# The last two stores of an attention and gating kernel in unequal shares of rows, on two queues

## The chip, the cores and the metric

The kernel runs on one core of a Trainium2 chip. The metric is device time in microseconds (us) for one execution, the median of several runs. Inputs and output lie in the chip's memory (HBM). A core has TensorE (matrix products, into PSUM), VectorE, ScalarE and GpSimd, and SyncE, which issues transfers; ScalarE and GpSimd can issue transfers too. The transfers of all queues are carried out by the core's 16 DMA engines.

## What is computed

Inputs are q, k and v of shape (4, 8, 768, 64), that is batch, heads, tokens, head width; a sort network of 8x8 values for each batch and head; and the weights of a gated block. The reference, cut to what matters:

```python
for _ in range(5):                       # P starts as sort_net
    P = exp(P - max(P, -1))
    P = P / (sum(P, -1) + 1e-9)
    P = P / (sum(P, -2) + 1e-9)
k_sorted, v_sorted = P applied to the 8 blocks of 96 tokens of k and v
attn = softmax(q_block @ k_sorted_block.T / 8)
x = (attn @ v_sorted_block), heads side by side     # (4, 768, 512)
h = relu(x @ w_in); u, v = the two halves of h      # 512 columns each
v_n = (v - mean(v)) / sqrt(var(v) + 1e-6)
v_s = w_spatial @ v_n + b_spatial                   # mixes the tokens
out = (u * v_s) @ w_out                             # (4, 768, 512), float32
```

## The kernel before

The work is cut into 360 units with short names (`VP`, `SP`, `OP` and so on), each a small function `u_XX`. A string, `ORDER` (L18 to L51), lists them, and a loop at L776 calls them in that order. Each engine carries out its own instructions in the order in which they are emitted, and waits on semaphores for what it reads. The order is written out by hand; nothing is planned at run time. The batch elements are 0 to 3, and the units of neighbouring elements are interleaved.

The 768 tokens of one element are six tiles of 128 rows. The last product, `out`, goes through these units:

- For elements 0, 1 and 2 the tiles are handled in pairs. `OP` (L628) multiplies a pair into PSUM (L635), `OE` (L642) copies it to a buffer in SBUF by ScalarE (L115) or VectorE (L117), and `OS` (L648) stores the pair, 128 rows by two tiles by 512 columns of float32 (512 KB), by one transfer that SyncE issues (L650). There are nine pairs.
- For element 3, the last one, the tiles are handled singly, in parts. `SH` (L660) mixes the tokens (L665) and adds the bias (L671), `GH` (L673) multiplies by u (L678), `OH` (L680) multiplies by the output weights (L685), `OI` (L690) copies a tile, or half the columns of one, out of PSUM (L115 on ScalarE, L117 on VectorE), and `OJ` (L695) stores it (L697). A store of 512 columns is 256 KB, one of 256 columns 128 KB. Tiles 4 and 5 go in two halves of 256 columns. The last stores in the order are tile 1, the second half of tile 4, and tile 0.

The buffers for the pairs and for the single tiles come from one pool of eight (`ld`, L99), which the loads of q, k and v use before. The function `queue` (L108) chooses the issuer: `A` is ScalarE, `S` is SyncE. In the traces the transfers of SyncE are queue q1 and those of ScalarE q10; q8 and q14 fetch instructions.

On SyncE other things stand between the stores: the copies from `vm` to `vb` (L423), four transposes of `x` into `xT` (`XD`, L506), and a load of a flag from SBUF (L721). At the end of the program SyncE waits until all transfers have landed (L807).

Of the kernel before, what the change touches and what calls it, by code (L numbers as in the profile page):

```python
# [38 lines left out]
VP:3:A:2:2:3 AT:1:3:3:1 GT:P:1:0 VP:2:A:2:0:1 ST:2:3 AT:1:3:2:1 AT:3:3:1:1 UP:0:A:2:1:1 OP:1:1:0 ST:2:0 ST:2:1 ST:2:2  # L39
OE:A:1:0 AT:2:3:0:1 LN:2:0:6 LA:2:1 UP:0:D:2:0:0 SC:1:3:0:0 LA:2:3 SC:3:3:1:0 LA:2:2 LA:2:5 LA:2:0 OP:2:1:4 AT:1:3:0:0  # L40
AT:3:3:1:0 XD:3:1 OE:A:1:4 OP:0:1:2 LA:2:4 SC:1:3:3:0 OE:D:1:2 SC:3:3:2:0 SP:2:2:2 AT:1:3:2:0 UP:0:A:2:0:1 AT:3:3:3:0
CK VP:2:A:3:4:5 GT:D:2:2 OS:1:2 SP:1:2:1 ST:3:5 OS:1:4 XD:3:0 SP:3:2:3 SP:2:2:0 ST:3:4 CF:3 GT:D:2:1 GT:P:2:3
UP:0:A:3:1:0 VP:2:D:3:2:3 VP:3:A:3:0:1 ST:3:0 ST:3:1 ST:3:2 UP:2:A:3:0:1 GT:P:2:0 LF OP:1:2:2 ST:3:3 OE:A:2:2 LN:3:0:6
OP:0:2:0 LA:3:4 LA:3:5 OS:2:2 OE:A:2:0 UP:3:D:3:1:1 LA:3:2 LA:3:0 OP:2:2:4 LA:3:3 OE:A:2:4 LA:3:1 OS:2:4 UP:0:A:3:0:0
SH:1:3:3:0 GH:P:3:3:0 SH:2:3:0:0 GH:D:3:0:0 SH:0:3:1:0 SH:2:3:2:0 SH:3:3:1:1 GH:P:3:1:0 SH:1:3:0:1 GH:P:3:2:0 OS:1:0
GH:P:3:1:1 SH:2:3:3:1 SH:3:3:2:1 OH:1:3:2:0:512:0:4 OS:2:0 GH:P:3:0:1 GH:D:3:2:1 GH:D:3:3:1 OH:2:3:3:0:512:0:4 OS:0:4
OH:0:3:4:0:256:0:4 OI:A:3:2:0:512 OI:A:3:3:0:512 OH:3:3:5:0:256:0:4 OI:D:3:4:0:256 OI:D:3:5:0:256 OJ:3:2:0:512:S
OJ:3:3:0:512:S OJ:3:4:0:256:S OJ:3:5:0:256:A OH:2:3:5:256:512:0:4 OH:1:3:1:0:512:0:4 OH:3:3:4:256:512:0:4
OI:D:3:5:256:512 OI:A:3:1:0:512 OJ:3:5:256:512:S OI:A:3:4:256:512 OJ:3:4:256:512:S OJ:3:1:0:512:A OH:2:3:0:0:512:0:4
OI:A:3:0:0:512 OJ:3:0:0:512:S  # L50
"""  # L51


# [12 lines left out]
def kernel(  # L66
# [12 lines left out]
    nc = tc.nc  # L79

    B, H, S, D = q.shape
    NB = sort_net.shape[-1]
    BLK = S // NB
    G = S // 128
# [23 lines left out]
    def queue(eng):  # L108
        if "general" in st:
            return nc.gpsimd  # L110
        return nc.scalar if eng == "A" else nc.sync

    def copy(eng, out, in_):
        if eng == "A":
            nc.scalar.copy(out=out, in_=in_)  # L115
        else:
            nc.vector.tensor_copy(out=out, in_=in_)  # L117
# [37 lines left out]
    st = {}  # L155
    count = {"e": 0, "k": 0}

    def ld_tile(name):
        return ld.tile([128, H, G * D], BF16, name=name, tag="ld")
# [197 lines left out]
    def u_QP(eng, b, hp):  # L357

        b, hp = int(b), int(hp)
        if ("qp", b) not in st:  # L360
            st["qp", b] = ld_tile("qp").rearrange("p h c -> p (h c)").rearrange(
                "p (k g h d) -> p k g h d", k=HP, g=G, h=2)
        getattr(nc, {"P": "gpsimd", "D": "vector"}[eng]).tensor_copy(
            out=st["qp", b][:, hp].rearrange("p g h d -> p h g d"),
            in_=st["q", b][:, 2 * hp:2 * hp + 2].rearrange("p h (g d) -> p h g d", g=G),
        )

    def u_QX(b, lo, hi):
# [326 lines left out]
    def u_OJ(b, n, c0, c1, eng="S"):  # L695
        b, n, c0, c1 = (int(x) for x in (b, n, c0, c1))
        queue(eng).dma_start(out=out[b, n * 128:(n + 1) * 128, c0:c1], in_=st["o1", b, n, c0])  # L697

    def u_CK():
        nc.vector.memset(bad, 0.0)  # L700
        over = lambda col, rows, in_, op, bound, test: (
            nc.vector.tensor_reduce(out=ends[0:rows, col:col + 1], in_=in_, axis=AX.X, op=op),
            nc.vector.tensor_scalar(
                out=bad[0:rows, col:col + 1], in0=ends[0:rows, col:col + 1],
                scalar1=bound, scalar2=None, op0=test),
        )
        recs = rec_all.rearrange("p n h i -> p (n h i)")
        over(0, BLK, recs, ALU.max, 1.0 / SUM_LO, ALU.is_gt)
        over(1, BLK, recs, ALU.min, 1.0 / SUM_HI, ALU.is_lt)
        over(2, BH, first[:, 0:NB], ALU.max, SUM_HI, ALU.is_gt)  # L710
        over(3, BH, first[:, 0:NB], ALU.min, SUM_LO, ALU.is_lt)
        over(4, BH, first[:, NB:2 * NB], ALU.min, COL_LO, ALU.is_lt)
# [99 lines left out]
```

## Time and profile before

| what | value |
|---|---|
| median of 3 runs | 157.59 us |
| lowest, highest run | 157.57, 157.9 us |
| the profiled execution | 158.23 us |
| its span | 156.4 us |
| outside the span | 1.8 us |
| TensorE busy | 147.1 us (94%) |
| VectorE busy | 120.4 us (77%) |
| ScalarE busy | 81.5 us (52%) |
| GpSimd busy | 36.8 us (24%) |
| granted TensorE clock | 0.999 |

The span runs from the first to the last instruction of one profiled execution, and times inside it are counted from its start. A group's line gives the source line, the engine, the operation, the tiles that it writes and reads with their shapes, and the count. In a timeline the first two numbers are start and length. A transfer has an issue, the short time that the issuing engine's queue needs for it, and a landing, the time from that issue until the semaphore of the whole transfer has come. A transfer's packets are spread over the DMA engines; the row of "DMA" digits gives their mean busy share in 40 equal slices of the window, and "GB/s" what they moved. Packets carry no engine's number.

### The profile page before, as it was taken

To read this page: it belongs to the slowest core of one execution; us is meant where nothing else is said; L and a number is where in the kernel's file an instruction comes from. 1 tells how busy PE (TensorE), PEld (TensorE's weight loads), DVE (VectorE), ACT (ScalarE), POOL (GpSimd) and SP (SyncE) were. 2 spreads that over 40 slices of the span, in tenths; PEclk is the share of its full clock that TensorE was granted. 3 is DMA by queue.
4 is the path that set the end of the run, shared out by engine and by line. 5 is a ranking of instruction groups with operands and counts; after the bars stand their busy time and mean duration, and the time that the engine had idled before them with its cause. 6 is when DMAs were issued, how large, how long until landed. Compare 5 with 4: busy or idle time off the path is not lost.

```text
span 156.4 us, 3976 instructions
## 1 busy us (share of the span) xinstructions
PE 147.1 (94%) x1650; PEld 89.7 (57%) x1665; DVE 120.4 (77%) x270; ACT 81.5 (52%) x112; POOL 36.8 (24%) x43
## 2 busy tenths in 40 slices
PE   6998898989999999999999999999999999999970
PEld 2355776844686669557655465555565545555640
DVE  4778699849997798479898889899969796747530
ACT  3466898867889504876556034556443025540230
POOL 7923855624000040052000000400000340006500
PEclk9999999999999999999999999999999999999999
DMA  2999999999999999990026445600569300349082
GB/s 76 264 204 204 205 204 205 207 219 239 274 209 203 204 204 204 244 198 4 0 41 198 79 160 96 114 0 4 101 235 71 67 0 0 134 151 379 13 307 105
DMA packets 27653, 23.57 MB, mean 151 GB/s; under 512 B 7280, under 2 KB 24688, under 8 KB 27632
## 3 DMA queue, kind: packets, MB, share of 16 engines
q0 software_dynamic: 14352, 11.80, 47.6%
q1 hardware_dynamic: 12992, 11.10, 26.4%
q10 hardware_dynamic: 288, 0.39, 0.7%
q8 instruction: 14, 0.23, 0.6%
q14 instruction: 7, 0.06, 0.1%
HBM read 24.78 MB, written 6.29 MB: 199 GB/s over the span
## 4 chain that ended last, share of the span: by engine, by line
PE 91%; DVE 2%; ACT 2%; issue 1%; DVEq 0%; ACTq 0%
PE ps L609 15%; PE ps L597 14%; PE ps L554 13%; PE ps L635 10%; PE ps L226 7%; PE ps L488 5%; PE ps L665 5%; PE ps L442 4%; PE ps L383 4%; PE ps L314 4%; PE ps L685 3%; PE ps L410 2%; PE ps L518 2%; PE ps L531 1%; DVE kt L117 1%
## 5 line engine op out<-in xcount | busy, mean ns | idle before, releaser
L447 ACT ACTIVATE ex<-ps 96x768 bf16<-96x768 f32 x32 | 24.8, 805 | 8.7 <-PE ps L442 8.6
L625 POOL TENSOR_TENSOR gt<-z,u_sb 128x768 bf16<-128x768 f32 x6 | 9.8, 1641 | 79.0 <-DVE z L615 61.2
L609 PE MATMUL ps<-wspT,v_sb 128*128 128x384 bf16 x144 | 25.1, 326 | 0.0
L597 PE MATMUL ps<-xT,w_in_sb 128*128 128x384 bf16 x128 | 23.5, 326 | 0.0
L554 PE MATMUL ps<-w_in_sb,xT 128*128 128x512 bf16 x87 | 22.1, 380 | 1.2 <-issue 0.8
L496 DVE TENSOR_TENSOR x_sb<-ps,rec_all 96x512 bf16<-96x512 f32 x32 | 22.0, 687 | 1.1
L609 PEld LDWEIGHTS <-v_sb 128*128 128x128 bf16 x144 | 13.5, 98 | 8.9
L571 DVE BATCH_NORM_STATS2 stats<-v_sb 128x6 f32<-128x512 bf16 x24 | 16.3, 678 | 2.0 <-ACT v_sb L121 1.5
L115 ACT COPY o_sb<-ps 128x1024 f32<-128x1024 f32 (+2 forms) x12 | 9.7, 816 | 15.2 <-PE ps L685 10.2
L635 PE MATMUL ps<-w_out_sb,gt 128*128 128x512 bf16 x68 | 16.7, 379 | 0.2
L615 DVE TENSOR_TENSOR z<-ps,b_bc 128x768 f32<-128x768 f32 x12 | 11.4, 952 | 7.0 <-PE ps L609 6.8
L121 ACT ACTIVATE u_sb<-ps 128x768 bf16<-128x768 f32 x12 | 9.7, 810 | 13.1 <-PE ps L597 13.0
L597 PEld LDWEIGHTS <-w_in_sb 128*128 128x128 bf16 x128 | 11.6, 98 | 7.4
L554 PEld LDWEIGHTS <-xT 128*128 128x128 bf16 x96 | 8.6, 98 | 10.0 <-issue 1.0
L121 ACT ACTIVATE v_sb<-ps 128x1024 bf16<-128x1024 f32 (+1 forms) x9 | 8.8, 976 | 9.4 <-PE ps L554 9.4
L488 PEld LDWEIGHTS <-ex 96*128 96x128 bf16 x256 | 10.6, 97 | 3.5
L488 PE MATMUL ps<-vb,ex 96*128 96x65 bf16 x256 | 12.1, 193 | 0.0
L226 PE MATMUL ps<-warm 128*128 128x512 bf16 x35 | 10.6, 460 | 1.3 <-DVE warm L199 1.3
L635 PEld LDWEIGHTS <-gt 128*128 128x128 bf16 x72 | 6.7, 98 | 7.2
L115 ACT CAST kt<-ps 128x768 bf16<-128x768 f32 x9 | 6.9, 800 | 6.5 <-PE ps L383 6.5
L442 PE MATMUL ps<-qT,kt 64*128 64x96 bf16 x256 | 9.3, 204 | 0.5 <-DVE kt L117 0.4
L442 PEld LDWEIGHTS <-kt 64*128 64x128 bf16 x256 | 6.2, 94 | 5.8 <-issue 3.9
(94 smaller groups left out, 208.2 us busy)
## 6 DMA issues: line engine op xcount, KB each, us to landing
out_dram<-o_sb SPq DMA_DIRECT2D x9, 512.0 KB, 3.6
k_in<-in_k_dram POOLq DMA_DIRECT2D x4, 768.0 KB, 23.3
v_in<-in_v_dram POOLq DMA_DIRECT2D x4, 768.0 KB, 22.4
vb<-vm SPq DMA_DIRECT2D x24, 99.0 KB, 5.8
q_in<-in_q_dram POOLq DMA_DIRECT2D x3, 768.0 KB, 29.6
ws_in<-in_moe_w_spatial_dram POOLq DMA_DIRECT2D x2, 576.0 KB, 22.8
w_in_sb<-in_moe_w_in_dram POOLq DMA_DIRECT2D x2, 512.0 KB, 24.1
q<-in_q_dram SPq DMA_DIRECT2D x1, 768.0 KB, 4.6
```

Source lines behind the costliest of these rows:

```text
L115: nc.scalar.copy(out=out, in_=in_)
L121: nc.scalar.activation(out=out, in_=in_, func=AF.Relu)
L226: nc.tensor.matmul(t[:, 0, 0:int(w)], lhsT=warm[:, 0:128], rhs=warm[:, 0:int(w)], start=True, stop=True)
L442: nc.tensor.matmul(t[:, hh, 0:HW].rearrange("p (g x) -> p g x", g=G)[:, :, ii * TB:(ii + 1) * TB], lhsT=kT[rows, i * BLK:i * BLK + 128], r ...
L447: nc.scalar.activation(out=e_tile(b, hp, ih).rearrange("p h (x g) -> p h x g", g=G), in_=t[0:BLK, :, 0:HW].rearrange("p h (g x) -> p h x g ...
L488: nc.tensor.matmul(t[:, hh, ii * VW:ii * VW + D + 1], lhsT=e[:, c:c + 128], rhs=vb[b % 2][:, ih * NI + ii, 2 * hp + hh, 0:D + 1], start=Tr ...
L496: nc.vector.tensor_mul(out=x_sb[:, hp].rearrange("p i (h d) -> p h i d", h=2), in0=tv[:, :, :, 0:D], in1=_raw_ap(rec, 0, [rec.ap[0], [NI, ...
L554: nc.tensor.matmul(t[:, x, :], lhsT=st["xT", b][:, n // 3, kc, (n % 3) * 128:(n % 3 + 1) * 128], rhs=w_in_sb[:, kc, DH:DFF], start=(kc == ...
L571: nc.vector.bn_stats(out=stats, in_=st["v_sb", b, n])
L597: nc.tensor.matmul(t[:, x, 0:HW], lhsT=w_in_sb[:, kc, mc * 128:(mc + 1) * 128], rhs=st["xT", b][:, ih, kc, :], start=(kc == 0), stop=(kc = ...
L609: nc.tensor.matmul(t[:, x, 0:HW], lhsT=st["v_sb", b, n][:, mc * 128:(mc + 1) * 128], rhs=wspT[:, 3 * x:3 * x + 3, n, :], start=(n == 0), s ...
L635: nc.tensor.matmul(t[:, x, :], lhsT=st["gt", b, mc][:, (n0 + x) * 128:(n0 + x + 1) * 128], rhs=w_out_sb[:, mc, :], start=(mc == 0), stop=( ...
```

## The change

Nothing of what is computed changes. In element 3, the second half of tile 4 is stored by two transfers, rows 0 to 99 by SyncE and rows 100 to 127 by ScalarE, and tile 0 by two, rows 0 to 119 by SyncE and 120 to 127 by ScalarE (new unit `OR`). The first half of tile 5 is now stored by SyncE, not ScalarE. The store of tile 1 by ScalarE stands ahead of ScalarE's copy of the second half of tile 4, and no longer behind it. Six of the nine pairs of elements 0 to 2 are stored by two transfers of SyncE, rows 0 to 119 and 120 to 127 of both tiles (new unit `OT`). The unit `QP`, which the order doesn't name, calls the helper `copy` now. The diff, with the lines of the order wrapped anew only left out where nothing else differs:

```diff
-CK VP:2:A:3:4:5 GT:D:2:2 OS:1:2 SP:1:2:1 ST:3:5 OS:1:4 XD:3:0 SP:3:2:3 SP:2:2:0 ST:3:4 CF:3 GT:D:2:1 GT:P:2:3
...
-OP:0:2:0 LA:3:4 LA:3:5 OS:2:2 OE:A:2:0 UP:3:D:3:1:1 LA:3:2 LA:3:0 OP:2:2:4 LA:3:3 OE:A:2:4 LA:3:1 OS:2:4 UP:0:A:3:0:0
-SH:1:3:3:0 GH:P:3:3:0 SH:2:3:0:0 GH:D:3:0:0 SH:0:3:1:0 SH:2:3:2:0 SH:3:3:1:1 GH:P:3:1:0 SH:1:3:0:1 GH:P:3:2:0 OS:1:0
-GH:P:3:1:1 SH:2:3:3:1 SH:3:3:2:1 OH:1:3:2:0:512:0:4 OS:2:0 GH:P:3:0:1 GH:D:3:2:1 GH:D:3:3:1 OH:2:3:3:0:512:0:4 OS:0:4
-OH:0:3:4:0:256:0:4 OI:A:3:2:0:512 OI:A:3:3:0:512 OH:3:3:5:0:256:0:4 OI:D:3:4:0:256 OI:D:3:5:0:256 OJ:3:2:0:512:S
-OJ:3:3:0:512:S OJ:3:4:0:256:S OJ:3:5:0:256:A OH:2:3:5:256:512:0:4 OH:1:3:1:0:512:0:4 OH:3:3:4:256:512:0:4
-OI:D:3:5:256:512 OI:A:3:1:0:512 OJ:3:5:256:512:S OI:A:3:4:256:512 OJ:3:4:256:512:S OJ:3:1:0:512:A OH:2:3:0:0:512:0:4
-OI:A:3:0:0:512 OJ:3:0:0:512:S
+CK VP:2:A:3:4:5 GT:D:2:2 OT:1:2:0:120 OT:1:2:120:128 SP:1:2:1 ST:3:5 OT:1:4:0:120 OT:1:4:120:128 XD:3:0 SP:3:2:3
...
+GT:P:2:0 LF OP:1:2:2 ST:3:3 OE:A:2:2 LN:3:0:6 OP:0:2:0 LA:3:4 LA:3:5 OT:2:2:0:120 OT:2:2:120:128 OE:A:2:0 UP:3:D:3:1:1
...
+SH:0:3:1:0 SH:2:3:2:0 SH:3:3:1:1 GH:P:3:1:0 SH:1:3:0:1 GH:P:3:2:0 OT:1:0:0:120 OT:1:0:120:128 GH:P:3:1:1 SH:2:3:3:1
+SH:3:3:2:1 OH:1:3:2:0:512:0:4 OT:2:0:0:120 OT:2:0:120:128 GH:P:3:0:1 GH:D:3:2:1 GH:D:3:3:1 OH:2:3:3:0:512:0:4
+OT:0:4:0:120 OT:0:4:120:128 OH:0:3:4:0:256:0:4 OI:A:3:2:0:512 OI:A:3:3:0:512 OH:3:3:5:0:256:0:4 OI:D:3:4:0:256
+OI:D:3:5:0:256 OJ:3:2:0:512:S OJ:3:3:0:512:S OJ:3:4:0:256:S OJ:3:5:0:256:S OH:2:3:5:256:512:0:4 OH:1:3:1:0:512:0:4
+OH:3:3:4:256:512:0:4 OI:D:3:5:256:512 OI:A:3:1:0:512 OJ:3:5:256:512:S OJ:3:1:0:512:A OI:A:3:4:256:512
+OR:3:4:256:512:S:0:100 OR:3:4:256:512:A:100:128 OH:2:3:0:0:512:0:4 OI:A:3:0:0:512 OR:3:0:0:512:S:0:120
+OR:3:0:0:512:A:120:128
...
+    def u_OT(b, n0, r0, r1):
+        b, n0, r0, r1 = (int(x) for x in (b, n0, r0, r1))
+        queue("S").dma_start(
+            out=out[b].rearrange("(c p) n -> p c n", p=128)[r0:r1, n0:n0 + 2, :], in_=st["o", b, n0][r0:r1])
+
+    def u_OR(b, n, c0, c1, eng, r0, r1):
+        b, n, c0, c1, r0, r1 = (int(x) for x in (b, n, c0, c1, r0, r1))
+        queue(eng).dma_start(out=out[b, n * 128 + r0:n * 128 + r1, c0:c1], in_=st["o1", b, n, c0][r0:r1])
```

More of the change, by code (lines that the diff above doesn't have):

```diff
@@ L41 @@
 AT:3:3:1:0 XD:3:1 OE:A:1:4 OP:0:1:2 LA:2:4 SC:1:3:3:0 OE:D:1:2 SC:3:3:2:0 SP:2:2:2 AT:1:3:2:0 UP:0:A:2:0:1 AT:3:3:3:0
-CK VP:2:A:3:4:5 GT:D:2:2 OS:1:2 SP:1:2:1 ST:3:5 OS:1:4 XD:3:0 SP:3:2:3 SP:2:2:0 ST:3:4 CF:3 GT:D:2:1 GT:P:2:3
-UP:0:A:3:1:0 VP:2:D:3:2:3 VP:3:A:3:0:1 ST:3:0 ST:3:1 ST:3:2 UP:2:A:3:0:1 GT:P:2:0 LF OP:1:2:2 ST:3:3 OE:A:2:2 LN:3:0:6
-OP:0:2:0 LA:3:4 LA:3:5 OS:2:2 OE:A:2:0 UP:3:D:3:1:1 LA:3:2 LA:3:0 OP:2:2:4 LA:3:3 OE:A:2:4 LA:3:1 OS:2:4 UP:0:A:3:0:0
-SH:1:3:3:0 GH:P:3:3:0 SH:2:3:0:0 GH:D:3:0:0 SH:0:3:1:0 SH:2:3:2:0 SH:3:3:1:1 GH:P:3:1:0 SH:1:3:0:1 GH:P:3:2:0 OS:1:0
-GH:P:3:1:1 SH:2:3:3:1 SH:3:3:2:1 OH:1:3:2:0:512:0:4 OS:2:0 GH:P:3:0:1 GH:D:3:2:1 GH:D:3:3:1 OH:2:3:3:0:512:0:4 OS:0:4
-OH:0:3:4:0:256:0:4 OI:A:3:2:0:512 OI:A:3:3:0:512 OH:3:3:5:0:256:0:4 OI:D:3:4:0:256 OI:D:3:5:0:256 OJ:3:2:0:512:S
-OJ:3:3:0:512:S OJ:3:4:0:256:S OJ:3:5:0:256:A OH:2:3:5:256:512:0:4 OH:1:3:1:0:512:0:4 OH:3:3:4:256:512:0:4
-OI:D:3:5:256:512 OI:A:3:1:0:512 OJ:3:5:256:512:S OI:A:3:4:256:512 OJ:3:4:256:512:S OJ:3:1:0:512:A OH:2:3:0:0:512:0:4
-OI:A:3:0:0:512 OJ:3:0:0:512:S
+CK VP:2:A:3:4:5 GT:D:2:2 OT:1:2:0:120 OT:1:2:120:128 SP:1:2:1 ST:3:5 OT:1:4:0:120 OT:1:4:120:128 XD:3:0 SP:3:2:3
+SP:2:2:0 ST:3:4 CF:3 GT:D:2:1 GT:P:2:3 UP:0:A:3:1:0 VP:2:D:3:2:3 VP:3:A:3:0:1 ST:3:0 ST:3:1 ST:3:2 UP:2:A:3:0:1
+GT:P:2:0 LF OP:1:2:2 ST:3:3 OE:A:2:2 LN:3:0:6 OP:0:2:0 LA:3:4 LA:3:5 OT:2:2:0:120 OT:2:2:120:128 OE:A:2:0 UP:3:D:3:1:1
+LA:3:2 LA:3:0 OP:2:2:4 LA:3:3 OE:A:2:4 LA:3:1 OS:2:4 UP:0:A:3:0:0 SH:1:3:3:0 GH:P:3:3:0 SH:2:3:0:0 GH:D:3:0:0
+SH:0:3:1:0 SH:2:3:2:0 SH:3:3:1:1 GH:P:3:1:0 SH:1:3:0:1 GH:P:3:2:0 OT:1:0:0:120 OT:1:0:120:128 GH:P:3:1:1 SH:2:3:3:1
[5 more added lines that the diff above has]
+OR:3:0:0:512:A:120:128
 """
@@ L362, in u_QP @@
                 "p (k g h d) -> p k g h d", k=HP, g=G, h=2)
-        getattr(nc, {"P": "gpsimd", "D": "vector"}[eng]).tensor_copy(
-            out=st["qp", b][:, hp].rearrange("p g h d -> p h g d"),
-            in_=st["q", b][:, 2 * hp:2 * hp + 2].rearrange("p h (g d) -> p h g d", g=G),
+        copy(
+            eng, st["qp", b][:, hp].rearrange("p g h d -> p h g d"),
+            st["q", b][:, 2 * hp:2 * hp + 2].rearrange("p h (g d) -> p h g d", g=G),
         )
```

## The prediction

> **What bounds the kernel now.** I read the page's head and chain first, then the last 16 us of the chain, then what SyncE waits for at the end, then the DMA table in narrow windows.
>
> ```profile
> span 156.4 us, 3976 instructions
> PE 91%; DVE 2%; ACT 2%; issue 1%; DVEq 0%; ACTq 0%
> ```
> ```profile
> 146.62 4.95 PE ps L685 x30
> 151.56 0.02 issue
> 151.58 0.58 ACT o_sb L115
> ```
> ```profile
> SPq L807 <- DMA out_dram<-o_sb: 1.7, 3, 1.0
> ```
>
> TensorE carries the chain to 151.56; the change touches no matmul. The last copy out of PSUM runs to 151.58 + 0.58 = 152.16. From there to the span's end at 156.4 are 4.24 us in which no engine computes: the last store is issued, moves and lands, and SyncE waits for it (L807). The change works on these 4.24 us. First the last store, then an early one of the same size:
>
> ```profile
> out_dram<-o_sb SPq DMA_DIRECT2D x1, 256.0 KB, 3.3
> L697 SPq DMA_DIRECT2D out_dram<-o_sb x1: 332/332/332, 152.2 to 152.2; - x1
> ```
> ```profile
> out_dram<-o_sb SPq DMA_DIRECT2D x1, 256.0 KB, 2.0
> L697 SPq DMA_DIRECT2D out_dram<-o_sb x1: 345/345/345, 147.9 to 147.9; - x1
> ```
>
> The first lands 2.0 us after its issue, the last 3.3 us after, at 152.2 + 3.3 = 155.5; another 0.9 us pass to 156.4. So 1.3 us of the end are lag. The stretches say whose (start:end, length, the five engines, clock, DMA share, GB/s):
>
> ```profile
> 151.90:153.00 1.10, 0.00 (x0) 0.00 (x0) 0.00 (x0) 0.27 (x1) 0.00 (x0) 1.00 0.91 317
> 153.00:153.80 0.80, 0.00 (x0) 0.00 (x0) 0.00 (x0) 0.00 (x0) 0.00 (x0) 1.00 0.90 323
> 153.80:155.10 1.30, 0.00 (x0) 0.00 (x0) 0.00 (x0) 0.00 (x0) 0.00 (x0) 1.00 0.08 32
> ```
>
> Until 153.8 the 16 DMA engines are 90% busy; then 0.08, which is 1.3 of 16. Closer, from 154.38 on:
>
> ```profile
> DMA  2000200002000200020000200020000200000000
> GB/s 114 0 0 0 114 0 0 0 0 114 0 0 0 114 0 0 0 114 0 0 0 0 114 0 0 0 114 0 0 0 0 114 0 0 0 0 0 0 0 0
> DMA packets 9, 0.02 MB, mean 23 GB/s; under 512 B 1, under 2 KB 1, under 8 KB 9
> ```
>
> Eight packets of 2 KB, 0.08 us apart, and a tiny one: that is one DMA engine (X below) doing alone its eight rows of the last store, 128 rows / 16. It ends at about 155.03; the landing at 155.5 is 0.47 later. Why X is late:
>
> ```profile
> q10 hardware_dynamic: 111, 0.20, 48.7%
> q1 hardware_dynamic: 138, 0.12, 34.1%
> q8 instruction: 1, 0.02, 5.9%
> q14 instruction: 1, 0.01, 2.1%
> ```
>
> In 151.9 to 153.0 one 16 KB fetch of instructions (q8) took 5.9% of 16 engines for 1.1 us: 1.04 us of one engine, in the middle of the stores. It delays by about as much as X is late. A second lag shows where the stores of the pairs end (144.6 to 145.4):
>
> ```profile
> GB/s 205 410 205 614 410 205 103 103 103 103 102 102 0 0 0 0 0 0 0 102 0 0 0 0 0 102 0 0 0 102 0 0 0 102 0 0 0 0 819 0
> q8 instruction: 1, 0.02, 7.5%
> ```
>
> Again one engine goes on alone from about 144.9, to 145.36, and the bin in which it ends (819) holds the next 16 KB fetch. I read this as the same X: its fetch starts as its stores are through. The inference is not proven by the rows, which carry no engine numbers.
>
> **The change part by part.** *The last store, 120 and 8 rows.* One engine has eight rows of a 128-row store (above), so 120 rows are 15 engines' worth, and 8 rows are one each for eight engines. If X is the one left out, its tail from 154.38 goes; if the 100 + 28 rows of the store before it also miss X, so do that store's rows, done before 154.38. The other engines were through at 153.8 and take one row more, 0.08 us. A sentence on the rule: the Trainium skill, DMA: Bandwidth & Descriptors, section "Why a DMA increments its semaphore by 16 and not by 1", says a copy from SP or ACT uses the largest number of engines up to 16 that divides its slowest dimension, and the lowest-numbered ones: 15, 8, 10 and 14 here, so engine 15 would get nothing of the last two stores. No row of before shows it. The section "Latency and other measured facts" of that page calls engines 7 and 15 the usually late ones; if X were 7, the first rival below would hold.
>
> *The order on ScalarE.* The copies and issues now:
>
> ```profile
> 150.76 0.38 ACT L115 COPY o_sb<-ps 128x256 f32<-128x256 f32 x1
> 150.90 0.34 ACTq L697 DMA_DIRECT2D out_dram<-o_sb  x1
> 151.58 0.58 ACT L115 COPY o_sb<-ps 128x512 f32<-128x512 f32 x1 [0.44 <-PE ps L685]
> ```
>
> The store of tile 1 stands behind the 256-column copy and is issued at 150.90 while that copy runs; ScalarE then idles 0.44 us for TensorE. After the change the order is copy 1, store 1, copy 4, share of store 4, copy 0. Store 1 waits for copy 1 as now: 150.90 + 0.34 = 151.24. Copy 4 is behind it: 151.24 + 0.38 = 151.62. The 28-row share waits for copy 4: 151.66 + 0.34 = 152.00. Copy 0 then starts at 152.00, not 151.58, ends at 152.58, and both shares of the last store are issued at 152.62, 0.42 later than now. That an issue holds back the next copy isn't shown by a row (the one above is followed by an idle wait anyway): bounds 0 and 0.42; the queue works in order, so I take 0.42. An issue of fewer rows may cost other than 0.33: by the store rows 0.33 to 0.40, so 0.07 at most; I take 0.33.
>
> *Landing.* An undisturbed 256 KB store took 2.0; I add 0.08 for the extra row: 152.62 + 2.08 = 154.7, 0.8 before the 155.5 of now. A floor stands beside it: the store of tile 1 stays at 128 rows, so X keeps its rows.
>
> ```profile
> out_dram<-o_sb ACTq DMA_DIRECT2D x1, 256.0 KB, 3.7
> L697 ACTq DMA_DIRECT2D out_dram<-o_sb x1: 338/338/338, 150.9 to 150.9; - x1
> ```
>
> It lands at 150.9 + 3.7 = 154.6 now and is still issued at 150.9. So what is late next is both at once, 154.6 and 154.7. If the fetch comes at another time the floor can fall to the undisturbed 154.2 to 154.3.
>
> *Store 3:5 moved from ScalarE to SyncE.* ScalarE idled there; SyncE has its next store 0.3 us later. I take 0, at most 0.07 for the store behind it, which is not the last.
>
> *Six pairs in 120 + 8.* Six more issues on SyncE. Its stores and what follows them there:
>
> ```profile
> 113.98 0.90 SPq L650 DMA_DIRECT2D out_dram<-o_sb  x2
> ```
> ```profile
> SPq L506 <- DVE ends L702: 4.3, 1, 4.3
> ```
> ```profile
> xT<-x_sb SPq DMA_TRANSPOSE x1, 5.3
> ```
> ```profile
> 124.54 1.47 PE L597 MATMUL ps<-xT,w_in_sb 128*128 128x384 bf16 x8
> ```
> ```profile
> 133.57 0.38 SPq L650 DMA_DIRECT2D out_dram<-o_sb  x1
> ```
> ```profile
> 138.32 3.11 SPq L650 DMA_DIRECT2D out_dram<-o_sb  x4
> 147.86 4.67 SPq L697 DMA_DIRECT2D out_dram<-o_sb  x6
> ```
>
> Two pairs at 113.98 become four issues, 0.9 longer. The transpose queued behind them (L506) waited 4.3 us for VectorE anyway; 3.4 are left. If it were late it would matter: it lands at 117.92 + 5.3 = 123.2 and TensorE reads xT at 124.54, so 1.3 us more are covered. The pair at 133.57 has 4 us to the next store. At 138.32 four issues become seven in a gap of 6.4 us before 147.86; at the longest of these issues (1.25, where the queue is backed up) three more are 3.7. Their bytes are the same; an engine with a double share takes 18 rows in place of 16 of each pair, an eighth more of 5 us, 0.6, landing near 146.5 where the buffer is next written at 148.1. So I cost the pairs at 0; each issue that lost its cover would cost 0.4. Their second store per buffer adds a wait to the copies that reuse it, with a satisfied count: below 0.05 each.
>
> *Sum.* Landing 155.5 to 154.7, -0.8 (last copy +0.42, lag -1.3, row +0.08); the 0.9 behind it stays. Span 155.6; the profiled execution would go from 158.23 (1.8 outside the span) to 157.4. The median of the runs is 0.64 below that execution; taking the same -0.8 from 157.59 gives **156.8**.
>
> **The rivals.** *The late engine is in the shares.* If X is one of the first eight, it gets 9 rows of the last store and 12 of the 1 KB rows before, in place of 8 and 8: one at 0.08 and four at about 0.04, +0.24. If its queue has also run dry by 153.4 (as when the fetch slips behind store 1), the 0.42 of the later copy is paid too with the old lag of 3.3. It decides from the moment that X's queue is empty when the last store arrives: 152.62 + 3.3 = 155.9, 157.59 + 0.42 = 158.0, with the rows 158.25; slower. For it: no row says which engine X is. Against: both tails are of one engine among sixteen with equal shares, first by 0.46 us and then by 1.2, and where all have eight rows I expect the one that is dealt the last rows, 120 to 127, to be the one that ends last; this is a guess from two tails, and my 0.73 below rests on it.
>
> *The shares change nothing.* The rows are still dealt to X. X would come to the last store at 154.38 as now, behind which the 0.42 hides, and end at 155.03: 157.6. The Trainium skill, same page, section "Rules for kernel authors", advises against this sort of split: two transfers on disjoint partitions use the same 16 engines, and several issuers save only issue time. The 16 engines 90% busy until 153.8 agree with it; the single engine after 153.8 speaks against its weight here, since no bandwidth is short there.
>
> *A neighbour takes over.* The stretch after 153.8 held 1.3 engines, so a second one was late too, by about 0.4. With nine rows of the last store it would land at 155.1: 157.2. That lies in my forecast's range.
>
> **How the numbers follow.** Forecast (with the neighbour) 0.73, its own range 156.3 (landing 1.3 earlier, no delay) to 157.2. No change 0.13, at 157.6. Slower 0.14, at 158.0. A measurement here tells 0.2%, 0.3 us, from no change. Range 156.3 to 157.8: it takes in the forecast and no change and leaves the slower rival out.
>
> **What would show it.** Right: after the last copy the DMA share falls to zero with no stretch of one engine alone; the last stores land about 2.1 after issue; ScalarE's last copy starts near 152.0. Wrong: a lone engine with 2 KB packets past 154.4, or a landing still 3 us after the issue. The pairs' tail at 145 should lose its lone engine; if a gap of TensorE appears near 124.5 or 148, the pairs were not free. If the last copy still starts at 151.58, the issue on ScalarE held nothing back.

## The result and the profile after

The changed kernel takes longer: the ratio of its time to that of the kernel before is 1.0061, with a 95% interval of 1.0046 to 1.0076 (medians 158.83 and 157.64 us). One of the 13 executions of the changed kernel ran at a granted clock of 0.564 and took 251.38 us; it counts in the median and not in the ratio. A second measurement of the same kernel, among the experiments below, gave 1.0025 (1.0007 to 1.0043). So it loses 0.4 to 1.0 us; the forecast was a gain of 0.8.

The head of its page, then ScalarE's timeline at the end (start, length, engine, line, what; in brackets the idle time before):

```profile
span 156.7 us, 4003 instructions
```
```profile
150.27 0.58 ACT L117 COPY o_sb<-ps 128x512 f32<-128x512 f32 x1 [1.59 <-PE ps L687]
150.89 0.39 ACTq L699 DMA_DIRECT2D out_dram<-o_sb  x1
151.38 0.37 ACT L117 COPY o_sb<-ps 128x256 f32<-128x256 f32 x1 [0.52 <-ACT o_sb L117]
151.78 0.65 ACTq L708 DMA_DIRECT2D out_dram<-o_sb  x1
152.53 0.58 ACT L117 COPY o_sb<-ps 128x512 f32<-128x512 f32 x1 [0.78 <-DMA out_dram<-o_sb]
153.14 0.31 ACTq L708 DMA_DIRECT2D out_dram<-o_sb  x1
```

TensorE ends where it did, at 151.5. The copy of tile 0 starts at 152.53, not at 151.58. It stands behind the 28-row share's issue, 151.78 + 0.65 = 152.43; the release that the row names is a transfer whose semaphore ScalarE checks in between, for 0.02 us. That semaphore's earlier transfers had landed by 146.8, so the issue is what the copy waited out. The last chain of the same profile shows the steps that have entered it:

```profile
150.89 0.39 ACTq L699
151.28 0.05 issue
151.32 0.02 ACTq L117
151.34 0.04 issue
151.38 0.38 ACT o_sb L117
151.76 0.02 issue
151.78 0.65 ACTq L708
152.43 0.04 issue
152.47 0.02 ACTq L117
152.49 0.04 issue
152.53 0.58 ACT o_sb L117
```

ScalarE's issues (ACTq) are on the path that sets the end; before, TensorE was on it to 151.56. Then the last store, and the DMA stretches after it (the columns before the clock are the idle engines; the last two are DMA share and GB/s):

```profile
out_dram<-o_sb SPq DMA_DIRECT2D x1, 240.0 KB, 2.6
L708 SPq DMA_DIRECT2D out_dram<-o_sb x1: 338/338/338, 153.1 to 153.1; - x1
```
```profile
153.90:154.40 0.50, 0.00 (x0) 0.00 (x0) 0.00 (x0) 0.00 (x0) 0.00 (x0) 0.66 0.80 164
154.40:154.90 0.50, 0.00 (x0) 0.00 (x0) 0.00 (x0) 0.00 (x0) 0.00 (x0) 0.50 0.82 229
154.90:155.30 0.40, 0.00 (x0) 0.00 (x0) 0.00 (x0) 0.00 (x0) 0.00 (x0) 0.50 0.49 184
155.30:156.70 1.40, 0.00 (x0) 0.00 (x0) 0.00 (x0) 0.00 (x0) 0.00 (x0) 0.50 0.00 0
```

The long tail of one engine is gone: the share falls from 0.82 over 0.49 to nothing, and the landing takes 2.6, not 3.3. One reason is in the instruction fetch, in the stretch from 151.2 to 152.5:

```profile
q8 instruction: 1, 0.02, 5.7%
```

This is the same 16 KB packet as before, but it ran from 151.29 to 152.47 and was through 0.66 us ahead of the last store's issue. Before, it ran from 151.94 to 152.98 and ended 0.79 behind that issue.

But look at the speed. Before, a share of 0.90 moved 323 GB/s, 359 for a full share; here 0.80 moves 164 and 0.82 moves 229, 205 and 279 for a full share. The DMA engines are nearly as busy and move 0.57 to 0.78 as much for it.

So in these two profiles the last issue is 0.95 later and the landing 0.65 shorter: +0.3 net, 156.4 to 156.7. The medians differ by more. The profiled execution of before, 158.23, lies 0.6 above its median, that of the changed kernel 0.3 below its own. What makes the loss 0.4 us in one measurement and 1.0 in the other isn't settled.

### The profile page after: what moved, and what is told of

Same layout as the page of the kernel before. It is cut to its first block, busy times and chain, and to the rows that moved or that the text cites. A ratio compares the mean times of both kernels' runs of the same rounds, so it can differ in the third digit from the quotient of the medians.

```text
span 156.7 us, 4003 instructions
## 1 busy us (share of the span) xinstructions
PE 148.8 (95%) x1665; PEld 89.8 (57%) x1665; DVE 120.4 (77%) x270; ACT 81.7 (52%) x112; POOL 36.8 (23%) x43
## 4 chain that ended last, share of the span: by engine, by line
PE 90%; ACT 3%; DVE 3%; issue 1%; ACTq 1%; DVEq 0%
PE ps L611 15%; PE ps L599 14%; PE ps L556 14%; PE ps L637 10%; PE ps L228 7%; PE ps L667 5%; PE ps L490 5%; PE ps L444 4%; PE ps L385 4%; PE ps L316 4%; PE ps L687 2%; PE ps L412 2%; PE ps L520 2%; DVE x_sb L498 1%; PE ps L533 1%; ACT o_sb L117 1%
## 5 line engine op out<-in xcount | busy, mean ns | idle before, releaser
L556 PE MATMUL ps<-w_in_sb,xT 128*128 128x512 bf16 x96 | 22.8, 380 | 0.0
L228 PE MATMUL ps<-warm 128*128 128x512 bf16 x36 | 11.2, 479 | 1.3 <-DVE warm L201 1.3
L497 DVE RECIPROCAL rec_all<-ps 96x8 f32<-96x8 f32 x32 | 6.3, 196 | 4.3 <-PE ps L490 4.0
```

Of the source, the lines that this page charges most:

```text
L228: nc.tensor.matmul(t[:, 0, 0:int(w)], lhsT=warm[:, 0:128], rhs=warm[:, 0:int(w)], start=True, stop=True)
L556: nc.tensor.matmul(t[:, x, :], lhsT=st["xT", b][:, n // 3, kc, (n % 3) * 128:(n % 3 + 1) * 128], rhs=w_in_sb[:, kc, DH:DFF], start=(kc == ...
```

## Experiments

Three theories. A: the loss is the last copy behind ScalarE's issues. B: transfers on fewer than 16 engines move slowly. C: the six pairs cost it. Three more, X, D and S, came out of the traces; the expectations below say what they mean. A quoted text is what was expected before the run. The table counts from the end of TensorE's last matmul in each kernel's own profile, in us: the start of the last copy, the issue of the last store (its larger share), SyncE's last check of a transfer, the end of the span. "112+16" and the like are rows.

| kernel | last copy | last issue | last check | end | ratio, 95% interval |
|---|---|---|---|---|---|
| before | 0.04 | 0.65 | 3.92 | 4.88 | 1 |
| changed | 0.99 | 1.60 | 4.22 | 5.18 | 1.0061 (1.0046 to 1.0076) |
| g1_again | 0.99 | 1.60 | 4.22 | 5.17 | 1.0025 (1.0007 to 1.0043) |
| e1_last | 0.04 | 0.65 | 4.37 | 5.33 | 1.0020 (1.0011 to 1.0029) |
| e2_pairs | 0.04 | 0.65 | 3.98 | 4.93 | 1.0004 (0.9995 to 1.0012) |
| e3_whole4 | 0.12 | 0.73 | 3.61 | 4.56 | 1.0003 (0.9993 to 1.0012) |
| e4_order | 0.10 | 0.72 | 4.16 | 5.12 | 1.0013 (1.0002 to 1.0025) |
| f1_behind | 0.12 | 0.74 | 3.75 | 4.70 | 1.0009 (0.9997 to 1.0021) |
| f2_thirteen | 0.12 | 0.74 | 3.82 | 4.77 | 1.0002 (0.9992 to 1.0012) |
| f3_seven | 0.04 | 0.65 | 3.81 | 4.76 | 0.9992 (0.9981 to 1.0003) |
| f4_sixteen | 1.46 | 2.07 | 4.55 | 5.51 | 1.0042 (1.0027 to 1.0057) |
| g2_store1 | 0.05 | 0.86 | 3.57 | 4.52 | 0.9995 (0.9983 to 1.0006) |
| g3_112 | 0.04 | 0.65 | 3.81 | 4.77 | 0.9999 (0.9988 to 1.0009) |
| h1_relief | 0.05 | 0.84 | 3.86 | 4.81 | 0.9996 (0.9987 to 1.0006) |

**e1_last**: before, with the last store alone in shares.

```diff
-OJ:3:0:0:512:S
+OR:3:0:0:512:S:0:120 OR:3:0:0:512:A:120:128
```

> The kernel before with one part of the change: the last store (tile 0) in shares of 120 rows by SyncE and 8 rows by ScalarE. Theory A (the change loses because ScalarE's last copy waits behind two issues on its own queue; the shares themselves gain): the last copy stays at 151.6, no DMA engine is left alone with the last store's rows, the last store lands 2.1 to 2.6 us after its issue at 152.2, total 156.9 to 157.2. Theory B (transfers on fewer than 16 engines move slowly): the last copy at 151.6 too, but the landing takes 3.3 us or more, total 157.6 to 158.0. Theory C (the six pairs cost the time): the shares do nothing, 157.6.

Measured 1.0020, slower, though the copy is not late. The DMA table from 153.86 to 154.60 of its profile, and SyncE's wait at the end:

```profile
DMA  3000020002000200002000200020002000000000
DMA packets 10, 0.02 MB, mean 22 GB/s; under 512 B 2, under 2 KB 2, under 8 KB 10
```
```profile
SPq L816 <- DMA out_dram<-o_sb: 2.1, 1, 2.1
```

Eight packets of 2 KB from one engine alone, as before: the late engine has eight rows of the 120. It is not the one that is left out. (That it is the same engine as before can't be read, since packets carry no engine's number.) The landing is 3.3 again. And there is a new loss: SyncE waits 2.1 us in one piece, and the last check comes 0.42 after the landing (4.37 against 0.65 + 3.3 = 3.95). That made theory D, for f3_seven. The total, 158.0, is at the upper end of what theory B expected.

**e2_pairs**: before, with the six pairs in shares (`OS:1:2` to `OT:1:2:0:120 OT:1:2:120:128`, and so on).

> The kernel before with the six pairs stored as 120 and 8 rows and nothing else. Theories A and B: the issues are covered, 157.6. Theory C (the pairs cost it): 158.2 to 158.6, with a gap of TensorE or a late transpose before 146. If the pairs' lone engine at 145 goes, the engine that fetches instructions is the one left out by 120 rows.

Measured 1.0004: theory C falls. But one pair moves alone, with nothing beside it, in 133.5 to 136.5, and so gives the price of a share. First the kernel before, then e2_pairs, the same 256 rows of 2 KB:

```profile
DMA packets 272, 0.52 MB, mean 175 GB/s; under 512 B 16, under 2 KB 16, under 8 KB 272
q1 hardware_dynamic: 272, 0.52, 46.2%
```
```profile
DMA packets 279, 0.52 MB, mean 175 GB/s; under 512 B 23, under 2 KB 23, under 8 KB 279
q1 hardware_dynamic: 279, 0.52, 64.3%
```

The packets took 46.2% of 16 engines for 3 us whole, 64.3% as 120 and 8 rows: 64.3 / 46.2 = 1.39 times the DMA time for the same bytes; f3_seven has the same 64.3% there. Theory B has a size now. The tiny packets, one for each engine that takes part, are 16 before and 23 = 15 + 8 after. That is what the rule of the Trainium skill says that the prediction named (DMA: Bandwidth & Descriptors, "Why a DMA increments its semaphore by 16 and not by 1"); the trace agrees.

The expectation named a sign: the lone engine at the end of the pairs should go if 120 rows leave out the engine that fetches. It stayed. At a share of 0.07 and 0.06, one engine of sixteen still moves pairs after 146.4:

```profile
146.40:146.70 0.30, 0.30 (x3) 0.18 (x2) 0.27 (x2) 0.00 (x0) 0.19 (x1) 1.00 0.07 27
146.70:147.30 0.60, 0.60 (x5) 0.25 (x4) 0.54 (x2) 0.49 (x1) 0.00 (x0) 1.00 0.06 24
```

**e3_whole4**: the changed kernel with tile 4's second half stored whole.

```diff
-OR:3:4:256:512:S:0:100 OR:3:4:256:512:A:100:128
+OJ:3:4:256:512:S
```

> The changed kernel, but the second half of tile 4 is stored whole by SyncE, not as 100 and 28 rows; everything else stays. Theory A: only store 1 is left ahead on ScalarE, the last copy starts at about 151.75 instead of 152.53, total 0.7 to 0.8 under the changed kernel, 157.2 to 157.9. Theory B (few engines are slow): the last store still has 120 and 8 rows, so most of the loss stays, 158.2 or more. Theory C: 158.6.

Measured 1.0003. ScalarE's timeline:

```profile
150.21 0.39 ACTq L698 DMA_DIRECT2D out_dram<-o_sb  x1
150.70 0.86 ACT L116 COPY o_sb<-ps 128x256 f32<-128x256 f32 x2 [0.52 <-ACT o_sb L116]
151.59 0.55 ACTq L707 DMA_DIRECT2D out_dram<-o_sb  x1
```

The copies of tiles 4 and 0 run back to back again (x2, no gap). The one issue that is left ahead of the last copy costs 0.1. The second issue is gone, and with it the loss of the changed kernel, while the pairs and the 120 + 8 rows are kept. That fits theory A; but the shares of tile 4 are gone too, and f1_behind tells the two apart.

**e4_order**: before, with the new order and every store whole (`OJ:3:1:0:512:A OI:A:3:4:256:512 OJ:3:4:256:512:S`, and `OJ:3:5:0:256:S`).

> The kernel before with only the change of order: store 1 ahead of the copy of tile 4's second half on ScalarE, and the first half of tile 5 stored by SyncE; all stores whole. Theory A: the last copy starts at 151.75, 0.2 later, but the lone engine sets the end as before: 157.6 (157.5 to 157.8). Theories B and C: 157.6.

Measured 1.0013. The copy is 0.1 late, not 0.2, but the total, 157.9, is above the 157.5 to 157.8 expected. Its last store had an unusual issue:

```profile
L696 SPq DMA_DIRECT2D out_dram<-o_sb x1: 994/994/994, 152.1 to 152.1; - x1
```

0.99 against 0.33 for the same store before. I come back to this under f4_sixteen.

**f1_behind**: the changed kernel with the 28-row share issued behind the last copy.

```diff
-OR:3:4:256:512:A:100:128 OH:2:3:0:0:512:0:4 OI:A:3:0:0:512
+OH:2:3:0:0:512:0:4 OI:A:3:0:0:512 OR:3:4:256:512:A:100:128
```

> The changed kernel with one thing moved: ScalarE issues the 28-row share of tile 4 behind the copy of tile 0, not ahead of it. Every store has the same shares. Theory A (the issue holds back the copy): the last copy starts within 0.1 us of TensorE's last matmul as before, not 1.0 us after it, and the total falls by 0.8 to 1.0 from the changed kernel, to 157.5 to 157.8. Theory B (few engines are slow): the shares still cost it, 158.3 or more.

Measured 1.0009. Its timeline:

```profile
151.14 0.86 ACT L116 COPY o_sb<-ps 128x256 f32<-128x256 f32 x2 [0.53 <-ACT o_sb L116]
151.54 1.03 ACTq L707 DMA_DIRECT2D out_dram<-o_sb  x2
```

Same transfers, same shares, one instruction moved: the copies close up, and the two issues run beside the copy. This shows theory A without a change in what moves. The copy comes 0.87 earlier than in the changed kernel and the last check only 0.47, because the landing is 3.0 again and not 2.6. In time the run is 0.8 us under the changed kernel's first measurement and 0.25 under g1_again, where the two intervals overlap. The shares bring no gain either way.

**f2_thirteen**: f1_behind with the last store cut at row 104.

```diff
-OR:3:0:0:512:S:0:120 OR:3:0:0:512:A:120:128
+OR:3:0:0:512:S:0:104 OR:3:0:0:512:A:104:128
```

> As the kernel f1_behind, but the last store is cut at row 104, not 120: 104 rows by SyncE and 24 by ScalarE. Theory X (the DMA engine that fetches instructions is not reached by shares of 100, 28 or 104 rows but is reached by 120, as the packets of the first runs count): nothing of the last two stores is left to the late engine; the lone tail goes, 156.8 to 157.2. If the late engine is among the first thirteen, or if there is no such engine, 157.5 to 157.9.

Measured 1.0002: no gain. In the stretches of its profile no engine stays alone:

```profile
153.20:153.80 0.60, 0.00 (x0) 0.00 (x0) 0.00 (x0) 0.00 (x0) 0.00 (x0) 1.00 0.76 232
153.80:154.40 0.60, 0.00 (x0) 0.00 (x0) 0.00 (x0) 0.00 (x0) 0.00 (x0) 1.00 0.35 126
154.40:155.00 0.60, 0.00 (x0) 0.00 (x0) 0.00 (x0) 0.00 (x0) 0.00 (x0) 1.00 0.00 0
```

The end is a slope, not one engine's tail. That fits an X that 104 rows miss, but it doesn't show it: the 16 KB fetch also came 0.6 us earlier than in f1_behind, counted from TensorE's end. And 13 engines have ten rows each or eight, in slow packets, and end hardly sooner than X did (last check 3.82 against 3.92).

**f3_seven**: e1_last with seven pairs in shares, so that eight transfers are added, not one.

> The kernel before with the last store as 120 and 8 rows (as e1_last) and seven pairs as 120 and 8 rows, so that eight transfers are added and not one. Theory D (at the end SyncE waits for its transfers' semaphores in a fixed order, each check 0.06 us; with one added transfer the last store's semaphore stands eight checks ahead of the end, with eight added it stands last): 0.4 less than e1_last, 157.5 to 157.7. If the 0.3 of e1_last are due to the shares themselves, 158.0.

Measured 0.9992 against 1.0020 for e1_last, with the same last store: 0.44 us (0.2 to 0.7 by the two intervals), the size that theory D gave. SyncE's wait at the end is in three pieces again:

```profile
SPq L817 <- DMA out_dram<-o_sb: 1.9, 3, 1.1
```

In the traces SyncE makes twelve checks at the end, 0.06 us apart where nothing is waited for, in a fixed order, and the transfers take eight semaphores in turn, which the last eight checks read. One transfer more shifts the last store to a place with seven checks behind it, 7 x 0.06 = 0.42; eight more shift it back. The six pairs of the change, with its two more shares, make eight. These runs show no other use of them.

**f4_sixteen**: the changed kernel with tile 4 cut at row 112 (`OR:3:4:256:512:S:0:112 OR:3:4:256:512:A:112:128`).

> The changed kernel with the store of tile 4's second half cut at row 112, not 100: 112 and 16 rows, whose counts divide by sixteen. The order on ScalarE stays. If an issue by ScalarE takes longer for a share that doesn't fill sixteen engines, ScalarE's issue takes 0.34 instead of 0.65 us and the last copy comes 0.3 earlier, total 158.2 to 158.4 (less what the late engine's seven or eight rows add). If it takes longer because SyncE issues at the same moment, 0.65 stays, and the total is 158.5 to 158.9.

Measured 1.0042. ScalarE's timeline:

```profile
151.23 1.12 ACTq L707 DMA_DIRECT2D out_dram<-o_sb  x1
152.45 0.58 ACT L116 COPY o_sb<-ps 128x512 f32<-128x512 f32 x1 [1.25 <-issue]
```

Both expectations were missed: the issue took 1.12 and the copy came 1.46 after TensorE, not 0.7 or 1.0. The longer issue again moves the copy by as much, which is theory A once more. What sets an issue's length is left open: 0.28 to 1.12 for the shares at the end. The long ones, 1.12 here (16 rows on sixteen engines) and 0.99 in e4_order (128 rows), may wait for room on the late engine; that is argued and no run tests it. Nor is the other rival settled, that an issue is longer when the other queue issues at the same moment. In the changed kernel both pairs of shares were issued together:

```profile
L708 SPq DMA_DIRECT2D out_dram<-o_sb x2: 319/328/338, 151.8 to 153.1; - x2
L708 ACTq DMA_DIRECT2D out_dram<-o_sb x2: 308/478/648, 151.8 to 153.1; - x2
```

ScalarE's issue took 0.65 beside SyncE's first one, and 0.31 beside its second.

**g1_again**: the changed kernel once more.

> The changed kernel once more, unchanged, for a second trace of its end. Theory A: the last copy starts 0.9 to 1.5 us after TensorE's last matmul because ScalarE's issue of the 28-row share is ahead of it, whatever the rest does; total 158.4 to 158.8. If the first trace was an outlier, the copy starts within 0.3.

```profile
151.21 0.65 ACTq L707 DMA_DIRECT2D out_dram<-o_sb  x1
151.95 0.59 ACT L116 COPY o_sb<-ps 128x512 f32<-128x512 f32 x1 [0.78 <-DMA out_dram<-o_sb]
```

The same 0.65 and the same 0.99 after TensorE. The copy is late in the same way again; the total, 158.2, came out lower than expected.

**g2_store1**: before, with store 1 in 104 and 24 rows (`OR:3:1:0:512:A:0:104 OR:3:1:0:512:S:104:128`) and seven pairs in shares.

> The kernel before with store 1 (tile 1, not one of the last two) in shares of 104 rows by ScalarE and 24 by SyncE, and seven pairs as 120 and 8 so that the last store's semaphore stays last at the end. Theory X (the late engine is one that 104 rows don't reach): it has 8 rows of 2 KB less behind its fetch, its tail ends 0.4 to 0.6 earlier, 157.0 to 157.3. If relieving one engine is worth nothing because the split rows move slowly themselves: 157.5 to 157.8.

Measured 0.9995, no difference that can be told. Its stretches:

```profile
153.20:153.60 0.40, 0.00 (x0) 0.00 (x0) 0.00 (x0) 0.00 (x0) 0.00 (x0) 1.00 0.62 236
153.60:154.10 0.50, 0.00 (x0) 0.00 (x0) 0.00 (x0) 0.00 (x0) 0.00 (x0) 1.00 0.10 37
```

The end comes a third of a microsecond sooner in this profile (last check 3.57 against 3.92), though SyncE's issue of the 24 rows took 0.74 and put the last one off by 0.2. A gain of 0.3 in one trace and none in twelve runs: inconclusive.

**g3_112**: f3_seven with the last store cut at row 112 (`OR:3:0:0:512:S:0:112 OR:3:0:0:512:A:112:128`).

> The kernel f3_seven (last store in two shares, seven pairs in two) with the last store cut at row 112, not 120: both shares fill sixteen engines. Theory S (rows that are dealt in another way than 128 over sixteen move slowly): the 2 KB packets of the last store take well over the 84 ns of the whole store in both, mean 110 to 150, and the total is that of f3_seven, 157.4 to 157.8. If only a count under sixteen is slow: 84 to 90 ns here and 0.3 less, 157.1 to 157.4.

```profile
152.40:152.90 0.50, 0.00 (x0) 0.00 (x0) 0.00 (x0) 0.00 (x0) 0.00 (x0) 1.00 0.88 260
152.90:153.40 0.50, 0.00 (x0) 0.00 (x0) 0.00 (x0) 0.00 (x0) 0.00 (x0) 1.00 0.85 279
```

Between the two expectations: 260 / 0.88 = 295 and 279 / 0.85 = 328 GB/s for a full share, where the whole store has 323 / 0.90 = 359 and the changed kernel 205 and 279. A 2 KB packet of the last stores took 102 ns in the mean here, 114 in f3_seven and 91 in the kernel before. Filling sixteen engines helps, but a split store stays slower than a whole one, so theory B's few engines are not all of it. Why the rows move slowly is open. The total is that of before.

**h1_relief**: the last store whole, the two ahead of it in shares that miss X, six pairs in shares.

> The last store whole again (128 rows by SyncE); the two stores ahead of it in shares that miss the late engine: tile 1 as 104 rows by ScalarE and 24 by SyncE, the second half of tile 4 as 100 rows by SyncE and 28 by ScalarE, the last issued behind the copy of tile 0; six pairs in two, so that the last store's semaphore stays last. Theory X with theory S (the gain is in relieving the late engine while the last rows themselves move at 84 to 91 ns): 0.2 to 0.4 less than g2_store1, 157.1 to 157.3. If issues of shares eat it again (SyncE's of 24 rows took 0.74), 157.5 to 157.8.

Measured 0.9996. SyncE's issue of the 24 rows again took 0.73, and the end is that of before. The gain expected from relieving X didn't come. So no version here beats the kernel before by more than its interval.

## Why the prediction was wrong

**The sum.** Two terms of the forecast were mis-sized. The later copy cost 0.95 us where it took 0.42, and landing got shorter by 0.65 where it took 1.3, less 0.08 for a row. In the two profiles that turns -0.8 into +0.3. With only one of the two put right, a gain of 0.2 to 0.3 would have been left.

**What bounds the kernel, right.** The end is issue, movement and landing of the last stores, and one engine's tail of 1.2 us is in it. That this engine is the one that fetched stays an inference. The packets of the trace fit it: each begins 4 ns before the end of the one ahead of it on its engine, and followed back so, the last engine's row begins at 153.03, 0.05 after the fetch ended.

**The order on ScalarE: the term that was mis-sized.** The prediction took "0.42" for the later copy, from whole stores' issues of 0.34. The mechanism was right, an issue holds back the next copy (f1_behind, f4_sixteen), but it cost 0.95. The 28-row issue took 0.65, not 0.34, so the bound that the prediction gave for a smaller share, 0.07 more at most, failed by itself. Store 1's issue took 0.39, and copy 4 started at 151.38, not 151.24; and 0.10 lies between the issue and the copy. 0.42 + 0.31 + 0.14 + 0.10 = 0.97, and two steps between were 0.01 shorter each.

**The last store, 120 and 8 rows: half wrong.** "If X is the one left out, its tail goes" fails at its condition. e1_last shows a late engine with eight rows of the 120, and in e2_pairs the lone engine at the end of the pairs stayed. The guess under it, that the late engine is the one dealt rows 120 to 127, was not borne out. In the changed kernel the tail went all the same, since the fetch came earlier and the last store later. The first rival came closest: the late engine in the shares, and the later copy paid. (That it is one of the first eight, no run shows.) Its price for the copy was the same 0.42, too small, and its lag of 3.3 too long.

**Landing: mis-sized.** "152.62 + 2.08" took the packet time of a whole store. Landing took 2.6: the shares' rows move more slowly (0.57 to 0.78 of the speed in the changed kernel; e2_pairs, 1.39 times the DMA time). The lag fell by 0.65, not by 1.3, and part of that is only that the last store came so late that X's queue was through. The extra row was counted, the slower rows weren't. The Trainium skill's advice against splitting rows (DMA: Bandwidth & Descriptors, "Rules for kernel authors") points the right way, and the trace goes further: a split into 120 and 8 rows isn't just without gain, it costs 39% more DMA time. The Trainium skill, same page, section "The descriptor swizzle", says that in a transfer to 128 partitions each engine writes one port of SBUF; the stores here read it. That rows dealt in another way mix the ports, and are slow for it, is a guess; no run here shows ports.

**The floor of store 1, 154.6**: it landed at 150.9 + 3.4 = 154.3 and set nothing.

**Six pairs at 0: right.** 1.0004 in e2_pairs. They were to land near 146.5; in the changed kernel the stretch to 146.7 still moves some:

```profile
145.90:146.70 0.80, 0.80 (x7) 0.53 (x6) 0.57 (x2) 0.00 (x0) 0.80 (x2) 1.00 0.38 123
```

The path to it differed: not the double share of eight engines but 39% more DMA time in all, and a lone engine that in e2_pairs went on past 146.7. TensorE has no gap there, nor at the read of xT:

```profile
124.53 1.47 PE L599 MATMUL ps<-xT,w_in_sb 128*128 128x384 bf16 x8
```

**What lies behind the landing: 0.9 predicted, 0.95 measured.** e1_last and f3_seven show that this was luck: with one transfer more it is 1.4, and with eight more, as in the change, 0.95 again.

**The chances.** 0.73 rested on the place of X, which no row gave; the prediction said so itself. The range ended at 157.8 and left out the one rival that was slower.

## What to carry over

Before you cut a last store in two, put an issue's length on the queue of the engine that still has to compute: a store issued ahead of a copy holds that copy until its issue is through (0.65 and 1.12 us of issue here), and a store issued behind the copy doesn't. Price a split store by its own packets, not by those of a whole one. And where one added transfer changes the end by 0.4 us, look at the order in which the program's end checks its semaphores.

## What the runs showed of the hardware

- The same 512 KB in 120 and 8 rows took 1.39 times the DMA time of 128 rows (e2_pairs); 112 and 16 rows moved 295 to 328 GB/s for a full share (g3_112) where the whole store of the kernel before moved 359.
- An issue on SyncE or ScalarE took 0.33 to 0.41 us for the whole stores at the end, but 0.28 to 1.12 for shares (f1_behind, f4_sixteen) and once 0.99 for a whole one (e4_order).
- ScalarE's copy doesn't start until the issue ahead of it is through: 0.65 us of issue put it 0.99 behind TensorE (changed kernel, g1_again), 1.12 put it 1.46 behind (f4_sixteen), and with the issue behind it the copy came after 0.12 (f1_behind).
- The packet of a 16 KB fetch of instructions took about 1 us (1.04 in the kernel before, 1.18 in the changed one). That its engine is the one that finishes the stores last is inferred from the times.
- SyncE's checks at the end cost 0.06 us each where the last transfer isn't the last one checked; with seven of them behind it, e1_last took 0.44 us more than f3_seven.
